# K sums of four heads in one piece with zero-padded remaining rows, the q phase by token tiles, and one weight block queued earlier

## The chip, the cores and the metric

The kernel runs on one core of one Trainium2 chip. The metric is the device time of one execution in microseconds (us); the time before is the median of three runs. TensorE is called PE, ScalarE ACT, VectorE DVE, GpSimd POOL, and SyncE SP (here only a DMA queue).

## The reference

Three stages in float32 follow each other (factors on the inputs left out):

```python
def phi(x):                                   # x: 4 batches, 8 heads, 576 tokens, 64
    h = x @ omega.T - sum(x * x) / 2          # 128 features
    return exp(h - max(h)) / sqrt(128)
q_p, k_p = phi(q * s), phi(k * s)
kv  = einsum('bhsm,bhsd->bhmd', k_p, v)       # the K sums; z = k_p summed over tokens
x   = (q_p @ kv) / (q_p @ z + 1e-06)          # 2304 tokens x 512 after joining the heads
g   = softplus(x @ w_in)                      # 512 -> 2048
y   = g @ w_out                               # 2048 -> 512
out = ((y @ w1) * (y @ w2)) @ w3 @ w_out2     # 512 -> 1024 -> 1024 -> 512
```

The kernel multiplies `w3 @ w_out2` first and applies the product to the tokens.

## The kernel before

All matrices are split into a high and a low part (`hi`, `lo`, type fp32r), and a product is three matmuls (`mm3`, L88 on). The attention's own sums are plain float32 matmuls, of which each shows as two instructions in the trace.

**K phase** (the loop over `i` in `range(2 * B)`, eight blocks of one batch and four heads). For each of four token tiles `t` of 128 tokens, `k_feat` projects four heads (six matmuls of 256 columns with `omh`, `oml`, named for the parts of omega), DVE takes the maxima (`nmax`, L312) and ACT the exponentials into `kp` (L317). The 576 tokens of a batch leave 64 rows over; those of two batches lie together in one tile `kpr` of 128 rows, even batches in rows 0 to 63 and odd ones in rows 64 to 127. `kv_sum(i, h)` sums one head of block `i`: four token tiles, in column halves of 64 (`matmul_half`), so eight float32 matmuls `ps<-vt,kp` of 128 rows x 64 columns, and then two matmuls `ps<-vrest,kpr` of 64 rows x 64 columns. Two heads of block `i - 1` are summed after `t = 2` and two after `t = 3`. The sums of four heads share a bank of PSUM and are copied to `kv` by ACT (L353).

**q phase** (the loop over `u`, a unit of one token tile and four heads; 36 units, 18 tiles). A unit takes: `q_feat` (the projection, `ps<-omh,qt`; exponentials one unit later), `q_turn` of the unit three before (four transposes `ps<-ident,qp`, copied to `qpt` by ACT, L373), `q_num` of the unit four before (eight float32 matmuls `ps<-kv,qpt` of 128 x 64, then `den`, its reciprocal and `xt` on DVE, L388 to L392), and in every second unit `x_turn` of an earlier tile (four transposes `ps<-ident,xt`, copied to `xs` by ACT and stored to `xd`). Between them `step` takes work from one queue, `queue`: the splitting of the next stage's weights, and of its tokens once they are stored (`operands`: casts such as `xs2h` on ACT, L433, sums and low parts on DVE).

**After it** come the up product (`widen` with `Up1`), the down product (`down`), the second up product (`Up2`), the weight product (`fold`, whose eight folds of 24 matmuls of 512 columns each need one block of w3, `made["w3", j]`, and all eight blocks of wo) and the last product (`narrow`).

The order on each engine is not that of the code: a scheduler places instructions by priority and by its own estimate of when operands are there. Every engine then works in that order. POOL makes the low parts of K and q (`split`, L266).

Of the kernel before, what the change touches and what calls it, by code (L numbers as in the profile page):

```python
# [19 lines left out]
F32 = mybir.dt.float32  # L20
# [7 lines left out]
B, H, S, D = 4, 8, 576, 64  # L28
M = 128
NT = B * S  # L30
DM, FF1, FF2 = 512, 2048, 1024
KD, NF, NJ = DM // 128, FF1 // 128, FF2 // 128
KT = 4
# [1 line left out]
BIAS = 896 * 16 * TOP  # L35
PSUM = bass.MemoryType.PSUM
DRAM = bass.MemoryType.DRAM
LQ = 3
LN = 1
XSLACK = 2  # L40
HALF = 64
PRE = 1
QBUF = 3
# [1 line left out]
QLAG = 1  # L45
N = 384
# [4 lines left out]
NG = NJ // 4  # L51
WSLOTS = 18
AHEAD = 4
JOB_Q = 0.9
# [10 lines left out]
def body(ctx: ExitStack, tc: tile.TileContext, q, k, k_rest, v, v_rest, om_t, w_in, w_out, w12, w3, wo, out):  # L65
# [10 lines left out]
    def ps():  # L76
        return ps_.tile([128, 512], F32, tag="ps", name="ps")
# [10 lines left out]
    def matmul(o, a, b, start, stop, **kw):  # L88
        nc.tensor.matmul(out=o, lhsT=a, rhs=b, start=start, stop=stop, **kw)  # L89
# [144 lines left out]
    def step(rate):  # L234
        due[0] += rate
        while due[0] > 0:
            if not pump_one():
                due[0] = min(due[0], 2.0)
                break
            due[0] -= 1  # L240
# [43 lines left out]
    def load_v(i):  # L284
        if i < 2 * B:
            vt[i] = K_.tile([128, KT, 4, D + 1], F32, tag="vt", bufs=3, name="vt")
            nc.sync.dma_start(out=vt[i], in_=v[i])

    def load_q(t):
        if t < NT // 128:  # L290
            raw[t] = Q_.tile([128, 512], F32, tag="rawq", bufs=4, name="rawq")
            nc.sync.dma_start(out=raw[t], in_=q[t])

    def split_q(t):
        if t < NT // 128:
            if len(qbuf) < QBUF:
                qbuf.append(Q_.tile([128, 2, 512], FR, name=f"qt{len(qbuf)}"))
            qt = qbuf[t % QBUF]
            split(qt[:, 0, :], qt[:, 1, :], raw[t])
            qts[t] = qt.rearrange("p x (c t) -> p x c t", c=4)  # L300
# [20 lines left out]
    def flush(n):  # L321
        while len(waiting) > n:
            waiting.pop(0)()
# [13 lines left out]

    def matmul_half(o, a, b, start, stop):
        for c in range(0, a.shape[-1], HALF):
            matmul(o[c:c + HALF], a[:, c:c + HALF], b, start, stop)  # L340

    def kv_sum(i, h):
        b, g = divmod(i, 2)
        if h == 0:
            if g == 0:
                kvs[b] = Q_.tile([128, H, D + 1], F32, name=f"kv{b}")
            kacc[i] = ps()[:, 0:4 * (D + 1)].rearrange("p (h d) -> p h d", h=4)
        for t in range(KT):
            matmul_half(kacc[i][:, h, :], kps[i][:, t, h, :], vt[i][:, t, h, :], t == 0, False)
        r, o = 2 * (b // 2) + g, 64 * (b % 2)  # L350
        matmul_half(kacc[i][:, h, :], kpr[r][o:o + 64, h, :], vrest[o:o + 64, r, h, :], False, True)
        if h == 3:
            nc.scalar.copy(out=kvs[b][:, 4 * g:4 * g + 4, :], in_=kacc.pop(i))  # L353

    qp, qpt, xt = {}, {}, {}

    def q_feat(u):
        t, g = divmod(u, 2)
        p = project(lambda p: [qts[t][:, x, 2 * g + p, :] for x in range(2)])

        def exps():
            qp[u] = M_.tile([128, 4, M], F32, tag="m", name="qp")
            features(*p, qp[u])

        waiting.append(exps)
        flush(QLAG)

    def q_turn(u):
        tp = ps()
        for h in range(4):  # L370
            nc.tensor.transpose(tp[:, 128 * h:128 * h + 128], qp[u][:, h, :], ident)  # L371
        qpt[u] = M_.tile([128, 4, 128], F32, tag="m", name="qpt")
        nc.scalar.copy(out=qpt[u], in_=tp.rearrange("p (h t) -> p h t", h=4))  # L373

    def q_num(u):
        t, g = divmod(u, 2)
        nm = ps()
        nm = nm[:, 0:4 * (D + 1)].rearrange("p (h d) -> p h d", h=4)
        lo, hi = 128 * t, 128 * t + 128
        for h in range(4):  # L380
            a = lo
            while a < hi:
                b = a // S
                e = min(hi, (b + 1) * S)
                matmul_half(nm[a - lo:e - lo, h, :], qpt[u][:, h, a - lo:e - lo], kvs[b][:, 4 * g + h, :], True, True)
                a = e
        den = sm.tile([128, 4, 1], F32, tag="den", name="den")
        nc.vector.tensor_scalar(out=den, in0=nm[:, :, D:D + 1], scalar1=1e-6 * M, scalar2=None, op0=ALU.add)  # L388
        nc.vector.reciprocal(out=den, in_=den)
        if g == 0:  # L390
            xt[t] = M_.tile([128, H, D], F32, tag="m", name="xt")
        nc.vector.tensor_tensor(  # L392
            out=xt[t][:, 4 * g:4 * g + 4, :], in0=nm[:, :, 0:D],
            in1=den.to_broadcast([128, 4, D]), op=ALU.mult,
        )

    def x_turn(t):
        tp = ps()
        x = xt[t].rearrange("p h d -> p (h d)")
        for c in range(KD):  # L400
            nc.tensor.transpose(tp[:, 128 * c:128 * c + 128], x[:, 128 * c:128 * c + 128], ident)  # L401
        xs = M_.tile([128, KD, 128], F32, tag="m", name="xs")
        nc.scalar.copy(out=xs, in_=tp.rearrange("p (c t) -> p c t", c=KD))
        nc.sync.dma_start(out=xd[:, :, 128 * t:128 * t + 128], in_=xs)
# [234 lines left out]
    split(*om_s, om)  # L639
    split_k(1)  # L640
    load_v(0)
    vrest = K_.tile([128, B, 4, D + 1], F32, name="vrest")
    nc.sync.dma_start(out=vrest, in_=v_rest)
    load_k(2)
    split_k(2)
    load_v(1)
# [2 lines left out]
    for i in range(2 * B):  # L649
        for t in range(KT):  # L650
            k_feat(i, t)
            if t == 0:
                load_k(i + 4)
            if t == 0 and i > PRE:
                split_k(i + 1)
            if t >= 2 and i:
                kv_sum(i - 1, 2 * t - 4)
                kv_sum(i - 1, 2 * t - 3)
            if t == KT - 1 and i:
                load_v(i + 2)  # L660
            if i == 2 * B - 1 and t < 2:
                split_q(t)
        if i % 4 == 0:
            for g in range(2):
                k_feat_rest(i // 2 + g)
        if i >= 2 * B - 3:
            load_q(i - (2 * B - 3))
    load_q(3)
    nq = 2 * NT // 128
    ln = LQ + LN  # L670
    lx = ln + XSLACK
    xo = {}
    for x in win[:2]:
        x.queue = nc.sync
    queue += job_ops(win[:2])
    for u in range(nq + lx + 2):
        if u >= LQ and u - LQ < nq:
            q_turn(u - LQ)
        if u >= nq:
            flush(max(0, QLAG - 1 - u + nq))  # L680
        if u == LQ:
            for h in range(4):
                kv_sum(2 * B - 1, h)
            kstack.close()
            pools["X0"] = ctx.enter_context(tc.tile_pool(name="X0", bufs=28, side="right", reuse_waits="tile"))
        if u >= ln and u - ln < nq:
            q_num(u - ln)
        if u >= lx and (u - lx) % 2 == 0:
            if (u - lx) // 2 < NT // 128:
                x_turn((u - lx) // 2)  # L690
                for c in range(2):
                    if (u - lx) // 2 == 2 * N // 128 * (c + 1) + 1:
                        xo[c], ops = operands(c, xd, "X0")
                        queue += ops
        if u < nq:
            q_feat(u)
            if u % 2:
                split_q(u // 2 + 2)
                load_q(u // 2 + 4)
        step(JOB_Q)  # L700
    until(lambda: 0 in ready)
    qstack.close()

# [106 lines left out]
    def wo_ops():  # L810
        ops = []
        for i in range(NJ):
            if i < NJ - 1:
                ops += halves(wof[i], 1, 2, "X1", lambda name: xslot("X1", 512, FR, name), ("wo", i))
            else:
                ops += halves(wof[i], 1, 0, None, lambda name: spare[name == "lo"], ("wo", i))
        return ops

    def w3_ops(j):
        return halves(w3f[j], 2, 2, "J", jt, ("w3", j))  # L820
# [206 lines left out]
    def after_2(c):  # L1027
        if c == 0:
            until(lambda: not queue)
            xn[0], ops = last_operands(0)  # L1030
            a, b = wo_ops(), w3_ops(0)
            queue.extend(b[:2] + a[:15] + b[2:] + a[15:] + ops)
        elif c == 1:
            free["X0"] -= 4
            free["W"] += 4
        else:
            free["X0"] -= 14
            free["W"] += 14

    widen(Up2, w12_j, ("X1", "X0", "X0"), after_2, lambda: None)  # L1040
    rows = {}
    order = [4 * g + 2 * h + e for g in range(NG) for e in range(2) for h in range(2)]
    for n, j in enumerate(order):
        if n + 1 < NJ:
            queue[:0] = w3_ops(order[n + 1])
        rows[j] = fold(j)
        if n % 2:
            queue[:0] = w34_ops(n // 2, rows[order[n - 1]], rows[j])
# [72 lines left out]
```

## Time and profile before

| | |
|---|---|
| median of 3 runs | 839.15 us (838.91 to 839.45) |
| the profiled execution | 840.52 us, of which its span is 838.7 us |
| PE busy | 823.8 us, 98% of the span |
| DVE, ACT, POOL busy | 593.5, 443.8 and 43.1 us |
| granted PE clock | full speed in every slice |
| K phase, q phase | about 4 to 61 us and 61 to 148 us of the span |

Busy time counts a matmul from its start to a modelled end, so neighbouring matmuls overlap. What one costs in a stream is the distance between two starts; this is how durations on PE are read below. A bracket such as [0.56 <-ACT xs1h L433] gives the idle time of the engine before the row and what ended it.

### The profile page before, as it was taken

The page shows a single profiled execution, that of the slowest core. Times are in us where ns is not written, and L with a number is a line of the kernel's source. Part 1 is how long each engine was busy: PE and PEld are TensorE (multiplying, and loading weights), DVE is VectorE, ACT ScalarE, POOL GpSimd, SP SyncE. Part 2 cuts the span into 40 slices and gives each one's busy share as a digit, 9 for nine tenths or more (in the row PEclk, how much of TensorE's full clock was granted, in tenths as well). Part 3 has the DMA queues.
Part 4 walks back from the last instruction along what each step waited for, and adds up shares of the span by engine and source line. Part 5 has one row for each costly group of instructions (what it writes and reads, how often), then busy time and mean ns, then how long its engine had stood idle before and what let it go on. Part 6 is the DMA issues. An engine that isn't in the chain of part 4 may idle for free.

```text
span 838.7 us, 14602 instructions
## 1 busy us (share of the span) xinstructions
PE 823.8 (98%) x5520; PEld 761.9 (91%) x5520; DVE 593.5 (71%) x1005; ACT 443.8 (53%) x863; POOL 43.1 (5%) x35
## 2 busy tenths in 40 slices
PE   8999999999999999999999999999999999999998
PEld 6888888989999999888888889999999997789998
DVE  4667888978676576765648834798887876978772
ACT  5688989566555566755645523332333223663440
POOL 3522331000000000000000000000000000000000
PEclk9999999999999999999999999999999999999999
DMA  8632354466534566778996623446455547153312
GB/s 298 225 130 76 105 176 139 148 214 211 205 129 147 188 222 223 249 249 266 308 314 228 216 67 96 176 146 208 181 216 214 185 144 259 68 172 111 103 67 75
DMA packets 75702, 150.05 MB, mean 179 GB/s; under 512 B 7152, under 2 KB 44656, under 8 KB 75632
## 3 DMA queue, kind: packets, MB, share of 16 engines
q1 hardware_dynamic: 64544, 101.94, 36.1%
q10 hardware_dynamic: 11088, 47.18, 16.5%
q8 instruction: 43, 0.70, 0.4%
q14 instruction: 27, 0.22, 0.1%
HBM read 98.24 MB, written 50.86 MB: 178 GB/s over the span
## 4 chain that ended last, share of the span: by engine, by line
PE 83%; DVE 7%; DMA 5%; ACT 2%; issue 1%; SPq 0%; ACTq 0%; DVEq 0%
PE ps L89 81%; DMA xq<-xd 1%; DVE s L925 1%; PE ps L371 1%; DMA xq<-pd 1%; DMA w3f<-f 1%; PE ps L401 1%; DMA raw<-in_w_in 1%; DVE s L426 1%; DVE f L141 1%; DMA wh<-wof 1%; DMA gd<-c 0%; DVE c L478 0%; DVE u L478 0%; DVE nmax L312 0%
## 5 line engine op out<-in xcount | busy, mean ns | idle before, releaser
L89 PE MATMUL ps<-dlo,hi 128*128 128x512 f32 (+1 forms) x320 | 117.7, 368 | 0.0
L89 PE MATMUL ps<-dhi,lo 128*128 128x512 f32 (+1 forms) x320 | 117.7, 368 | 0.0
L89 PE MATMUL ps<-dhi,hi 128*128 128x512 f32 (+1 forms) x320 | 117.5, 368 | 0.0
L586 DVE TENSOR_TENSOR dlo<-dn,dhi 128x512 fp32r<-128x512 f32 (+1 forms) x80 | 50.3, 634 | 48.3 <-ACT dhi L585 30.3
L585 ACT CAST dhi<-dn 128x512 fp32r<-128x512 f32 (+1 forms) x80 | 45.5, 575 | 54.8 <-DVE dlo L586 29.8
L478 DVE TENSOR_TENSOR c<-ps,u 128x384 f32<-128x384 f32 x144 | 71.5, 549 | 0.8
L478 DVE TENSOR_TENSOR u<-ps,p 128x384 f32<-128x384 f32 x48 | 26.6, 555 | 61.7 <-PE ps L89 57.4
L89 PEld LDWEIGHTS ps<-dhi,hi 128*128 128x128 f32 x320 | 60.3, 189 | 10.1
L89 PEld LDWEIGHTS ps<-dlo,hi 128*128 128x128 f32 x320 | 60.3, 189 | 10.0
L89 PEld LDWEIGHTS ps<-dhi,lo 128*128 128x128 f32 x320 | 60.3, 189 | 9.9
L131 ACT ACTIVATE f<-raw,bias 128x1024 f32<-128x1024 int16 (+2 forms) x43 | 46.3, 1083 | 37.6 <-DMA w3f<-f 9.4
L312 DVE TENSOR_REDUCE nmax<-ps 128x4 f32<-128x512 f32 x72 | 48.4, 683 | 21.0 <-PE ps L89 10.5
L511 ACT ACTIVATE c<-c 128x384 f32<-128x384 f32 x72 | 35.2, 525 | 49.8 <-DVE c L478 49.8
L135 DVE SCALAR_TENSOR_TENSOR f<-raw,f 128x1024 int32<-128x1024 f32 (+2 forms) x43 | 45.0, 1048 | 20.5 <-ACT raw L132 20.4
L485 ACT COPY p<-ps 128x384 f32<-128x384 f32 x48 | 22.8, 475 | 60.9 <-PE ps L89 45.4
L132 ACT ACTIVATE raw<-raw,bias 128x1024 f32<-128x1024 int16 (+2 forms) x43 | 46.3, 1084 | 0.5
L141 DVE SCALAR_TENSOR_TENSOR f<-raw,f 128x1024 int32<-128x1024 int32 (+2 forms) x43 | 46.0, 1069 | 0.5
L317 ACT ACTIVATE qp<-ps,nmax 128x128 f32<-128x128 f32 x144 | 41.8, 396 | 3.3 <-DVE nmax L312 3.1
L317 ACT ACTIVATE kp<-ps,nmax 128x128 f32<-128x128 f32 x128 | 35.4, 419 | 13.0 <-DVE nmax L312 12.9
L89 PE MATMUL ps<-omh,qt 128*128 128x256 f32 x144 | 34.7, 305 | 0.0
L89 PE MATMUL ps<-xs1h,thi 128*128 128x384 f32 x96 | 32.3, 336 | 1.2 <-DVE c L478 0.6
L89 PE MATMUL ps<-xs2l,thi 128*128 128x384 f32 x96 | 32.2, 335 | 0.6 <-DVE xs2l L436 0.6
(227 smaller groups left out, 2282.5 us busy)
## 6 DMA issues: line engine op xcount, KB each, us to landing
dn<-gd SPq DMA_DIRECT2D x64, 256.0 KB, 4.0
raw<-in_w ACTq DMA_DIRECT2D x16, 1023.8 KB, 6.3
gd<-c SPq DMA_DIRECT2D x80, 192.0 KB, 2.8
pd<-c SPq DMA_DIRECT2D x48, 192.0 KB, 2.5
raw<-in_w_out ACTq DMA_DIRECT2D x10, 767.8 KB, 4.3
raw<-in_w_in ACTq DMA_DIRECT2D x6, 1023.8 KB, 5.2
rawq<-in_q SPq DMA_DIRECT2D x18, 256.0 KB, 3.3
xd<-xs SPq DMA_DIRECT2D x18, 256.0 KB, 3.0
```

Of the source, the lines that this page charges most:

```text
L89: nc.tensor.matmul(out=o, lhsT=a, rhs=b, start=start, stop=stop, **kw)
L131: nc.scalar.activation(out=self.f, in_=top, func=AF.Relu, scale=TOP, bias=bias[:, 0:1])
L132: nc.scalar.activation(out=self.words(1, F32, 2), in_=top, func=AF.Identity, scale=TOP, bias=bias[:, 1:2])
L135: nc.vector.scalar_tensor_tensor(out=self.f.bitcast(I32), in0=self.words(1, F32, 2), scalar=-2.0 ** 31, in1=self.f, op0=ALU.max, op1=ALU.min)
L141: nc.vector.scalar_tensor_tensor(out=fi, in0=self.words(0, I32, 2), scalar=13, in1=fi, op0=ALU.logical_shift_right, op1=ALU.bitwise_or,)
L312: nc.vector.tensor_reduce(out=nmax, in_=pj, axis=AX.X, op=ALU.max, negate=True)
L317: nc.scalar.activation(out=dst[:, h, :], in_=pj[:, h, :], func=AF.Exp, bias=nmax[:, h:h + 1])
L478: nc.vector.tensor_tensor(out=z, in0=bank, in1=y, op=ALU.add)
L485: nc.scalar.copy(out=p6, in_=b1)
L511: nc.scalar.activation(out=dst, in_=src, func=AF.Softplus)
L585: nc.scalar.copy(out=hi, in_=got[m])
L586: nc.vector.tensor_tensor(out=lo, in0=got.pop(m), in1=hi.bitcast(F32), op=ALU.subtract)
```

## The change

It has three parts. (1) `kv_sum(i)` sums all four heads of a block at once, after `t = 3`, as one accumulation group of the bank. `vrest` gets a copy for each parity of the batch in which the other parity's 64 rows are zero (two POOL memsets and two DMAs of 64 rows in place of one of 128), and the remaining rows are then multiplied with all 128 rows. (2) The q phase goes by whole token tiles: turns of the tile two before between the two projections, then both `q_num` of that tile, then `x_turn` of the tile three before. (3) The second w3 block of the weight product is queued with the first, behind all of wo; the loop no longer puts it at the queue's head.

```diff
-LQ = 3
-LN = 1
-XSLACK = 2
+TLAG = 2
+XLAG = 3
...
-            matmul(o[c:c + HALF], a[:, c:c + HALF], b, start, stop)
-
-    def kv_sum(i, h):
+            matmul(o[c:c + HALF], a[:, c:c + HALF], b, start, stop, skip_group_check=True)
+
+    def kv_sum(i):
         b, g = divmod(i, 2)
...
+        acc = ps()[:, 0:4 * (D + 1)].rearrange("p (h d) -> p h d", h=4)
+        for h in range(4):
+            for t in range(KT):
+                matmul_half(acc[:, h, :], kps[i][:, t, h, :], vt[i][:, t, h, :], h == 0 and t == 0, False)
+            r = 2 * (b // 2) + g
+            matmul_half(acc[:, h, :], kpr[r][:, h, :], vrest[:, b % 2, r, h, :], False, h == 3)
+        nc.scalar.copy(out=kvs[b][:, 4 * g:4 * g + 4, :], in_=acc)
...
-    vrest = K_.tile([128, B, 4, D + 1], F32, name="vrest")
-    nc.sync.dma_start(out=vrest, in_=v_rest)
+    vrest = K_.tile([128, 2, B, 4, D + 1], F32, name="vrest")
+    for x in range(2):
+        nc.gpsimd.memset(vrest[64 * (1 - x):64 * (2 - x), x], 0.0)
+        nc.sync.dma_start(out=vrest[64 * x:64 * x + 64, x], in_=v_rest[64 * x:64 * x + 64])
...
-            if t >= 2 and i:
-                kv_sum(i - 1, 2 * t - 4)
-                kv_sum(i - 1, 2 * t - 3)
             if t == KT - 1 and i:
+                kv_sum(i - 1)
                 load_v(i + 2)
...
-    for u in range(nq + lx + 2):
-        if u >= LQ and u - LQ < nq:
-            q_turn(u - LQ)
...
+    for t in range(nt + XLAG):
+        for g in range(2):
+            if 0 <= t - TLAG < nt:
+                q_turn(2 * (t - TLAG) + g)
+            if t < nt:
+                q_feat(2 * t + g)
+            else:
+                flush(0)
+            step(JOB_Q)
+        if t < nt:
+            split_q(t + 2)
+            load_q(t + 4)
+        if t == 1:
+            kv_sum(2 * B - 1)
...
+        if 0 <= t - TLAG < nt:
+            for g in range(2):
+                q_num(2 * (t - TLAG) + g)
+        if t >= XLAG:
+            x_turn(t - XLAG)
...
-            a, b = wo_ops(), w3_ops(0)
-            queue.extend(b[:2] + a[:15] + b[2:] + a[15:] + ops)
+            a, b = wo_ops(), w3_ops(order[0])
+            queue.extend(b[:2] + a[:15] + b[2:] + a[15:] + w3_ops(order[1]) + ops)
...
-        if n + 1 < NJ:
+        if 0 < n < NJ - 1:
             queue[:0] = w3_ops(order[n + 1])
```

How the instructions move on PE in the K phase: first the end of a block before (`omh,kt2h` and the like are the projection, `vt,kp` and `vrest,kpr` the sums of two heads; each row counts matmuls).

```order
L89 MATMUL ps<-omh,kt2l 128x256
L89 MATMUL ps<-vt,kp 64x65 x8
L89 MATMUL ps<-vrest,kpr 64x65 x2
L89 MATMUL ps<-vt,kp 64x65 x8
L89 MATMUL ps<-vrest,kpr 64x65 x2
L89 MATMUL ps<-omh,kt2h 128x256
```

Now the sums of four heads stand together behind the fourth projection of a block. In the block with `kt2`, though, the scheduler put one `vt,kp` by itself among the projections, and moved the matmuls with the low part `kt2l` behind those with `kt2h`:

```order
L88 MATMUL ps<-omh,kt2h 128x256
L88 MATMUL ps<-oml,kt2h 128x256
L88 MATMUL ps<-vt,kp 64x65
L88 MATMUL ps<-omh,kt2l 128x256
L88 MATMUL ps<-omh,kt2h 128x256
L88 MATMUL ps<-oml,kt2h 128x256
L88 MATMUL ps<-omh,kt2l 128x256 x2
```

So PE turns from projections to sums once in a block instead of twice, and once more in that block for the single matmul.

On PE in the q phase, one tile before (`ident,qp` and `ident,xt` are the transposes, `kv_282,qpt` the sums of `q_num`):

```order
L371 MATMUL ps<-ident,qp 128x128 x4
L89 MATMUL ps<-kv_282,qpt 64x65 x8
L89 MATMUL ps<-omh,qt_994 128x256
L89 MATMUL ps<-oml,qt_994 128x256
L89 MATMUL ps<-omh,qt_994 128x256 x2
L89 MATMUL ps<-oml,qt_994 128x256
L89 MATMUL ps<-omh,qt_994 128x256
L371 MATMUL ps<-ident,qp 128x128 x4
L89 MATMUL ps<-kv_282,qpt 64x65 x8
L401 MATMUL ps<-ident,xt 128x128 x4
```

and with the change:

```order
L88 MATMUL ps<-omh,qt_880 128x256
L88 MATMUL ps<-oml,qt_880 128x256
L88 MATMUL ps<-omh,qt_880 128x256 x2
L88 MATMUL ps<-oml,qt_880 128x256
L88 MATMUL ps<-omh,qt_880 128x256
L88 MATMUL ps<-kv_298,qpt 64x65 x16
L399 MATMUL ps<-ident,xt 128x128 x4
L369 MATMUL ps<-ident,qp 128x128 x4
```

The 16 sums of a tile now follow its second projection in one piece, and the second turn of the same tile stands only one projection ahead of them.

On ACT behind the q phase, where the operands of the third group of 768 tokens are cast (`xs3h`, `xs1h`) and the next weights are unpacked (`f<-raw`, whose `raw` a DMA brings), before:

```order
L485 COPY p_2800<-ps 128x384
L433 CAST xs3h<-s_2739 128x768
L131 ACTIVATE f<-raw,bias 128x1024
L433 CAST xs1h<-s_2717 128x768
L132 ACTIVATE raw<-raw,bias 128x1024
```

and with the change:

```order
L509 ACTIVATE c_2790<-ps 128x384
L483 COPY p_2803<-ps 128x384
L431 CAST xs1h<-s_2720 128x768
L130 ACTIVATE f<-raw,bias 128x1024
L431 CAST xa12h<-xq 128x768
```

The cast `xs1h` no longer stands behind the unpacking that waits for a DMA.

## Rows read from the trace of the kernel before

**Rows 1.** Windows: length, busy us of PE, PEld, DVE, ACT, POOL; clock, DMA share, GB/s.
```profile
18.98:61.34 42.36, 42.36 (x637) 37.21 (x633) 26.37 (x38) 33.60 (x118) 16.11 (x9) 1.00 0.54 183
76.28:86.71 10.43, 9.22 (x114) 7.72 (x113) 10.36 (x27) 7.40 (x24) 1.80 (x2) 1.00 0.36 102
86.71:108.27 21.56, 21.56 (x281) 19.20 (x280) 17.55 (x49) 19.08 (x56) 7.20 (x6) 1.00 0.50 149
108.27:118.37 10.10, 9.54 (x114) 7.83 (x113) 8.48 (x22) 9.58 (x27) 2.39 (x2) 1.00 0.63 208
118.37:139.97 21.60, 21.60 (x282) 19.17 (x281) 19.23 (x50) 20.79 (x60) 5.36 (x4) 1.00 0.34 100
```

**Rows 2.** The chain that ended last, from its one long piece on PE.
```profile
174.55 451.47 PE ps L89 x2424
```

**Rows 3.** Timeline of PE, K phase: start us, us, engine, line, operation, instructions.
```profile
21.23 0.28 PE L89 MATMUL ps<-omh,kt2l 128*128 128x256 f32 x1
21.44 0.69 PE L89 MATMUL ps<-vt,kp 128*64 128x65 f32 x16
22.06 0.33 PE L89 MATMUL ps<-vrest,kpr 64*64 64x65 f32 x4
22.32 0.69 PE L89 MATMUL ps<-vt,kp 128*64 128x65 f32 x16
...
23.20 0.39 PE L89 MATMUL ps<-omh,kt2h 128*128 128x256 f32 x1
23.42 0.28 PE L89 MATMUL ps<-oml,kt2h 128*128 128x256 f32 x1
23.54 0.28 PE L89 MATMUL ps<-omh,kt2l 128*128 128x256 f32 x1
```

**Rows 4.** Timeline of POOL: its one 128x128 memset, and the second K split.
```profile
0.73 0.20 POOL masks.py:197 MEMSET ident<- 128x128 f32 x1 [0.29 <-POOLq L1109]
...
16.92 2.36 POOL L266 TENSOR_TENSOR kt2l<-rawk,kt2h 128x1024 fp32r<-128x1024 f32 x1 [2.38 <-DVE kt2h L265]
```

**Rows 5.** Timeline of PE: the first turn among the last K sums, first and last.
```profile
63.56 0.33 PE L371 MATMUL ps<-ident,qp 128*128 128x128 f32 x1
...
66.03 0.69 PE L89 MATMUL ps<-vt,kp 128*64 128x65 f32 x16
```

**Rows 6.** Timeline of PE, q phase: a return to the projection, and the last tiles.
```profile
131.95 0.39 PE L89 MATMUL ps<-omh,qt 128*128 128x256 f32 x1
132.17 0.28 PE L89 MATMUL ps<-oml,qt 128*128 128x256 f32 x1
...
142.55 0.66 PE L401 MATMUL ps<-ident,xt 128*128 128x128 f32 x4
143.04 0.60 PE L371 MATMUL ps<-ident,qp 128*128 128x128 f32 x4
...
145.39 0.66 PE L401 MATMUL ps<-ident,xt 128*128 128x128 f32 x4
145.98 0.69 PE L89 MATMUL ps<-kv,qpt 128*64 128x65 f32 x16
148.23 0.44 PE L401 MATMUL ps<-ident,xt 128*128 128x128 f32 x2 [1.56 <-DVE xt L392]
```

**Rows 7.** Timeline of ACT: one tile of the q phase with a cast.
```profile
138.20 0.96 ACT L433 CAST xa22h<-xq 128x768 fp32r<-128x768 f32 x1
...
142.52 1.23 ACT L317 ACTIVATE qp<-ps,nmax 128x128 f32<-128x128 f32 x4
```

**Rows 8.** Timeline of PE: the last wait ahead of the long piece.
```profile
174.55 0.45 PE L89 MATMUL ps<-xs1h,thi 128*128 128x384 f32 x1 [0.56 <-ACT xs1h L433]
```

**Rows 9.** Timeline of SP's queue and of ACT: second w3 block, last wo block.
```profile
699.78 0.93 SPq L785 DMA_DIRECT2D wh<-w3f  x2
700.75 0.43 SPq L785 DMA_DIRECT2D wh<-wof  x1
...
705.20 0.62 ACT L794 CAST spare<-wh 128x512 fp32r<-128x512 f32 x1 [0.87 <-DMA wh<-wof]
```

More of the change, by code (lines that the diff above doesn't have):

```diff
@@ L339, in matmul_half @@
         for c in range(0, a.shape[-1], HALF):
-            matmul(o[c:c + HALF], a[:, c:c + HALF], b, start, stop)
-    def kv_sum(i, h):
+            matmul(o[c:c + HALF], a[:, c:c + HALF], b, start, stop, skip_group_check=True)
+    def kv_sum(i):
         b, g = divmod(i, 2)
[L344 to L353, printed above, removed]
+        if g == 0:
+            kvs[b] = Q_.tile([128, H, D + 1], F32, name=f"kv{b}")
+        acc = ps()[:, 0:4 * (D + 1)].rearrange("p (h d) -> p h d", h=4)
[5 more added lines that the diff above has]
+        nc.scalar.copy(out=kvs[b][:, 4 * g:4 * g + 4, :], in_=acc)
     qp, qpt, xt = {}, {}, {}
@@ L668, in body @@
     load_q(3)
-    nq = 2 * NT // 128
-    ln = LQ + LN
-    lx = ln + XSLACK
     xo = {}
@@ L675, in body @@
     queue += job_ops(win[:2])
-    for u in range(nq + lx + 2):
-        if u >= LQ and u - LQ < nq:
-            q_turn(u - LQ)
[L679 to L683, printed above, removed]
+    nt = NT // 128
+    for t in range(nt + XLAG):
[12 more added lines that the diff above has]
+            kv_sum(2 * B - 1)
             kstack.close()
             pools["X0"] = ctx.enter_context(tc.tile_pool(name="X0", bufs=28, side="right", reuse_waits="tile"))
[L686 to L700, printed above, removed]
+        if 0 <= t - TLAG < nt:
[3 more added lines that the diff above has]
+            x_turn(t - XLAG)
+            for c in range(2):
+                if t - XLAG == 2 * N // 128 * (c + 1) + 1:
+                    xo[c], ops = operands(c, xd, "X0")
+                    queue += ops
     until(lambda: 0 in ready)
@@ L1038, in after_2 @@
             free["W"] += 14
+    order = [4 * g + 2 * h + e for g in range(NG) for e in range(2) for h in range(2)]
     widen(Up2, w12_j, ("X1", "X0", "X0"), after_2, lambda: None)
     rows = {}
-    order = [4 * g + 2 * h + e for g in range(NG) for e in range(2) for h in range(2)]
     for n, j in enumerate(order):
-        if n + 1 < NJ:
+        if 0 < n < NJ - 1:
             queue[:0] = w3_ops(order[n + 1])
```

## The prediction

> **What bounds the kernel now.** I read the page first (98% of the span is PE), then the chain of waits. From 174.55 us on the chain is one piece of matmuls, 451 us long [rows 2]: what PE saves ahead of that point arrives whole at its end, and the diff touches nothing between there and the weight product. So the question is how fast PE gets through the K and q phases. The windows [rows 1] part them. In the K phase PE is busy all of the 42.36 us, ACT for 33.6 and DVE for 26.4: PE alone sets the pace. In the q phase, windows are cut where the sums of a tile's second unit start. Five tiles take 21.56 us (86.71 to 108.27) and five 21.60 (118.37 to 139.97), 4.32 a tile, with PE never idle; but ACT is busy for 19.08 and then 20.79 of it. Two windows of two tiles take 10.43 and 10.10 in place of 8.64: 1.79 and 1.46 lost, the first with DVE busy for 10.36.
>
> Within a phase I read starts on PE's timeline. In [rows 3] two projections start 0.12 apart (23.42 to 23.54); sixteen `vt,kp` instructions take 0.62, 0.039 each; four `vrest,kpr` take 0.26 where four of the others would take 0.155. Going from projections to sums costs 0.21 - 0.12 = 0.09 (21.23 to 21.44), going back 0.22 - 0.12 = 0.10 (23.20 to 23.42). The kernel pays for changes of shape, and the change makes fewer of them.
>
> **Part by part.** The sum is made against the profiled execution, 840.52 us; the median is 839.15, so 1.37 is taken off at the end.
>
> *Remaining rows with 128 rows.* Same instructions, same columns, but now of the shape of their neighbours. 32 heads x (0.26 - 0.155) = -3.4 [rows 3]. Ends: 0 if the 0.26 is not due to the 64 rows, -3.4.
>
> *Four heads in one piece.* Seven blocks (those summed inside the loop) lose one way out and back, 0.19: -1.3 [rows 3]. Ends -1.0 to -1.5, by the reading error of a start.
>
> *Memsets, the DMA and the single matmul.* No row has a memset of 64x1040. The bounds are the one of 128x128, 0.20, and the 128x1024 subtraction, 2.36 [rows 4]; I take 1, below the middle, since the first is the same kind of instruction. POOL has 2.38 idle ahead of the `kt2l` split, so either end is hidden there. The second DMA only takes a place in SP's queue some 11 us before what follows is used. But DVE now casts `kt2h` one maximum (0.61) later, so `kt2l` is ready at 16.92 + 0.6 + 2.36 = 19.9. PE begins this block at 18.98 (where the first window of [rows 1] is cut), 0.61 earlier by the two terms above, has eight projections and the single matmul to do and gets to `kt2l` about 19.5: a wait of 0.4. With the single `vt,kp` (a way out and back, 0.2): +0.6. Ends +0.2 and +1.2.
>
> *The first turn out of the last K sums.* From 63.56 to 66.03 [rows 5], 2.47, lie four transposes (at most 0.49, [rows 6], 142.55 to 143.04), 16 `vt,kp` (0.62) and 4 `vrest,kpr` (0.26): 1.10 went on crossings between them. One way out and back stays: -0.9. Ends -0.6 to -1.1.
>
> *q phase by tiles.* Before, a tile goes twice from transposes to sums (0.59 - 0.49 = 0.10, [rows 6]), once from sums to projections (131.95 to 132.17, 0.10) and once from sums to transposes; with the change once from projections to sums (0.09) and once to transposes. Per tile 0.30 - 0.09 = 0.21. Only where PE sets the pace does this come out. A tile with a cast takes 4.32 on ACT, one instruction behind the other (138.20 to 142.52, [rows 7]), which is what it takes on PE; ACT's new order has a cast in each of the four tiles near the end of the phase, so these gain nothing. Of the four disturbed tiles the first two are DVE's (10.36 of 10.43): nothing. In the other two DVE is not full (8.48 of 10.10), and `x_turn` now comes two units behind its `xt` instead of one, so I let half of the 1.46 go: -0.7. Ten tiles x 0.21 = -2.1. Together -2.8; ends 0 (ACT everywhere) and -3.8 - 3.25 = -7.0 (PE everywhere, disturbances gone).
>
> *End of the phase.* The last two tiles have no projections left to cover the copies of their turns; the row at 148.23 shows 1.56 idle there already, for `xt` [rows 6]. I put these equal. Behind it, `xs1h` no longer waits behind the unpacking of weights on ACT: the 0.56 of [rows 8] goes, -0.5. Ends -0.9 and +1.2 (one transpose-and-copy more for each of two tiles, 0.6 each).
>
> *Weight product.* The three transfers are issued at the same three places of the queue; the last wo block moves up by 0.97 and the w3 pair back by about 0.45 [rows 9]. The first fold, which needed the wo block (cast at 705.20), ends earlier, the second starts later. Taken as 0; ends -1.0 and +0.5.
>
> Sum: -3.4 - 1.3 + 0.6 - 0.9 - 2.8 - 0.5 + 0 = -8.3. Profiled: 832.2; median: 839.15 - 8.3 = **830.9**.
>
> **Rivals.** *Disturbances absorbed* (chance 0.18). Turns run three units behind their exponentials instead of two, `x_turn` two behind `xt`: enough for DVE's bursts. For it: in 86.71 to 108.27 DVE is at 81% without PE ever waiting. Against: DVE's 10.36 of 10.43. All 18 tiles gain (-3.8) and most of the 3.25 goes (-2.6): -11.9, 827.2.
>
> *ACT sets the pace of the q phase* (0.20). Its 20.79 of 21.60 us [rows 1] speaks for it, 19.08 of 21.56 against. The phase gains nothing: -5.5, 833.6.
>
> *The remaining rows are not cheaper* (0.08). Then the 0.26 comes from the change of operands and not from the 64 rows; PE's 0.10 for other changes of shape speaks against: -4.9, 834.2. The Trainium skill ("TensorE: Matmul & The Clock Gate", Part 3) goes further: products on different row or column groups run at the same time, so the two halves of a small product would overlap and padding would throw this away. By that rule four instructions take two steps, an estimate of 0.078, padding costs 32 x 0.077 = 2.5, and the time is 836.7. The trace disagrees: 0.26 is more than four steps, not fewer.
>
> *Slower* (0.04): the sums of a tile now need the copy of a turn that stands one projection ahead of them, where they had a whole unit before. If ACT reaches that copy late in each tile, because exponentials in front of it wait for DVE's maxima, each tile loses what a disturbed one loses now, (1.79 + 1.46) / 4 = 0.8. The q term is then 18 x 0.8 - 3.25 = +11.2 in place of -2.8, the sum +5.7 and the time 844.9. It decides from 5.5 / 18 = 0.3 us a tile. Against it: ACT is idle for 2.5 of 21.56 us in the first quiet window, so it is seldom that late.
>
> **How the numbers follow.** The forecast's case has 0.50. A measurement of this kernel can tell 0.2%, 1.7 us. All cases but the last lie over 1.7 below 839.15: 0.94 faster; 0.02 same, for a forecast or rival whose bounds all fall high; 0.04 slower. The range reaches from the absorbed case with a little of its lower bound (826.0) to the unchanged q phase with `kt2l` and the tail at their dear ends (836.0).
>
> **What would show it.** In the profile after: four `vrest,kpr` in 0.155 us (the first term); blocks of the K phase 0.6 shorter; the end of the K phase some 4 us earlier; quiet tiles of 4.1 in the q phase and 4.3 where ACT has a cast; the long piece on PE starting near 166. It is wrong if tiles stay at 4.3 throughout with ACT full, if four `vrest,kpr` still take 0.26, or if PE waits for `qpt` ahead of the sums in most tiles.

## The result, and the profile after

The changed kernel takes 832.1 us (median of 4 runs, 831.43 to 832.73), beside 839.03 us of the kernel before in the same session: the ratio is 0.9919 (95% interval 0.9902 to 0.9937), so 6.8 us less. The profiled execution took 832.73 us with a span of 830.9 us, 7.8 less than the 838.7 before. The forecast for the median was 830.9, 8.3 less. The total is nearly right, but the two profiles show that its parts are not.

The first view is that of the windows, cut where the same matmuls start in both kernels: the K phase from the first projection with `kt1h` to the first q projection, and the q phase to the first matmul of the up product (the columns are those of [rows 1]). With the change:

```profile
10.82:53.12 42.30, 41.38 (x738) 39.22 (x736) 29.33 (x43) 35.26 (x128) 21.77 (x14) 1.00 0.74 263
53.12:140.03 86.91, 77.28 (x1091) 71.11 (x1087) 76.53 (x190) 80.76 (x226) 21.59 (x15) 1.00 0.40 120
```

And the same two in the kernel before:

```profile
12.00:61.34 49.34, 49.34 (x739) 43.32 (x737) 31.90 (x47) 39.22 (x140) 20.72 (x13) 1.00 0.60 213
61.34:148.42 87.08, 83.75 (x1090) 72.51 (x1087) 71.79 (x184) 77.40 (x215) 20.59 (x15) 1.00 0.40 121
```

This K phase takes 42.30 instead of 49.34 us, 7.0 less, where the forecast had about 3.6 by that point (28 of the 32 heads at 0.105, 1.3 for the crossings, 0.6 back at `kt2l`). The first q projection starts 8.2 earlier (53.12 instead of 61.34), but 1.2 of that lay already at the first projection with `kt1h`, ahead of every sum. In the ten profiles with this K part that projection starts anywhere from 10.39 to 11.92, while the way from it to the first q projection takes 42.3 to 42.6 in all of them: the 7.0 belong to the kernel, the 1.2 can belong to the execution. The q phase, from which the forecast took another 4 or so, takes 86.91 instead of 87.08. In it PE works 6.5 us less (83.75 to 77.28), and 6.3 of that are idle time now.

Why K gained so much stands on PE's timeline of the changed kernel, at the last four heads:

```profile
56.17 0.69 PE L88 MATMUL ps<-vt,kp 128*64 128x65 f32 x16
56.68 0.29 PE L88 MATMUL ps<-vrest,kpr 128*64 128x65 f32 x4
56.80 0.64 PE L88 MATMUL ps<-vt,kp 128*64 128x65 f32 x16
57.27 0.29 PE L88 MATMUL ps<-vrest,kpr 128*64 128x65 f32 x4
57.38 0.64 PE L88 MATMUL ps<-vt,kp 128*64 128x65 f32 x16
```

Four `vrest,kpr` take 0.12 now (56.68 to 56.80), as forecast or a little less. But the sixteen `vt,kp`, whose instructions did not change at all, take 0.51 and then 0.47, where they took 0.62 [rows 3]. Four heads go from twice 1.76 us (21.44 to 23.20 in [rows 3]) to 2.48 (56.17 to 58.65, where the next transpose starts). A block is 1.2 shorter (29.31 to 34.85, 5.54; before 32.60 to 39.36, 6.76), except two: that with `kt2`, where PE waits 0.74 for `kt2l` and goes out and back once more, gains 0.1 (16.57 to 23.35; before 18.98 to 25.86), and the next one, where it waits 0.19 for `kt1l`, gains 0.8 (to 29.31; before to 32.60).

The waits show what the q phase does with what it won. PE's waits after (what it waited for, us in total, times, longest):

```profile
PE ps L88 <- ACT qpt L371: 7.6, 12, 1.7
PE ps L88 <- DMA rawk<-in_k: 4.0, 1, 4.0
PE ps L399 <- DVE den L387: 1.8, 1, 1.8
PE ps L88 <- DVE c L476: 1.8, 2, 1.5
PE ps L88 <- ACT hi L790: 1.2, 1, 1.2
PE ps L88 <- POOL kt2l L265: 0.7, 1, 0.7
```

The first row is new: the sums wait for the copy of their own tile's turn, 12 times. On PE's timeline these waits lie in three places, at the entry (62.88, 64.40), in the middle where operands are loaded (103.69 among others), and in the last tiles:

```profile
62.88 0.69 PE L88 MATMUL ps<-kv,qpt 128*64 128x65 f32 x16 [1.70 <-ACT qpt L371]
64.40 0.69 PE L88 MATMUL ps<-kv,qpt 128*64 128x65 f32 x16 [0.83 <-ACT qpt L371]
...
103.69 0.69 PE L88 MATMUL ps<-kv,qpt 128*64 128x65 f32 x16 [0.83 <-ACT qpt L371]
...
133.84 0.69 PE L88 MATMUL ps<-kv,qpt 128*64 128x65 f32 x16 [0.84 <-ACT qpt L371]
136.28 1.17 PE L88 MATMUL ps<-kv,qpt 128*64 128x65 f32 x32 [0.29 <-ACT qpt L371]
139.86 0.41 PE L399 MATMUL ps<-ident,xt 128*128 128x128 f32 x2 [1.82 <-DVE den L387]
```

ACT's timeline says why at the first two places. The transposes of the first turn run from 58.65 to 59.31, but their copy runs at 62.24, behind twelve exponentials, a weight cast and a copy of `kv` in ACT's order; and in the middle ACT stands for a DMA, with the copies of two finished transposes behind it:

```profile
57.61 3.29 ACT L316 ACTIVATE qp<-ps,nmax 128x128 f32<-128x128 f32 x12
61.02 1.04 ACT L179 CAST thi<-t 128x1024 fp32r<-128x1024 f32 x1
61.97 0.37 ACT L351 COPY kv<-ps 128x260 f32<-128x260 f32 x1
62.24 0.59 ACT L371 COPY qpt<-ps 128x512 f32<-128x512 f32 x1
...
100.31 0.83 ACT L431 CAST xa11h<-xq 128x768 fp32r<-128x768 f32 x1 [0.90 <-DMA xq<-xd]
101.05 0.58 ACT L401 COPY xs<-ps 128x512 f32<-128x512 f32 x1
101.53 0.59 ACT L371 COPY qpt<-ps 128x512 f32<-128x512 f32 x1
```

Last, the granted clock. It fell to 0.50 (1.2 GHz) behind the last of these waits: in the windows of the changed kernel PE idles for 1.82 of 137.40 to 140.00, and from about 140.6 on it runs three us at half speed.

```profile
137.40:140.00 2.60, 0.78 (x8) 0.58 (x7) 2.60 (x8) 1.17 (x2) 0.00 (x0) 1.00 0.23 65
141.00:144.00 3.00, 3.00 (x12) 2.90 (x11) 2.58 (x3) 1.99 (x4) 0.00 (x0) 0.50 0.00 0
```

Matmuls of the up product stand 0.32 apart there (140.63, 140.95, 141.27) instead of 0.17, and the lead over the kernel before falls from 8.4 us at 140.03 to 6.9 at 143.94. It comes back to 9.0 by 175 us, because PE no longer waits for `xs2l` (0.60 idle before, the lead grows by 0.9 there) and `xs1h` (0.56, [rows 8], by 1.0 there); 1.4 are lost again by 638.78 at two waits for `c` in the down product.

### The profile page after: what moved, and what is told of

It reads as the page before. It is cut to its first block, busy times and chain, and to the rows that moved or that the text cites. A ratio compares the mean times of both kernels' runs of the same rounds, so it can differ in the third digit from the quotient of the medians.

```text
span 830.9 us, 14593 instructions
## 1 busy us (share of the span) xinstructions
PE 808.8 (97%) x5520; PEld 757.2 (91%) x5520; DVE 595.9 (72%) x1005; ACT 443.7 (53%) x863; POOL 46.1 (6%) x37
## 5 line engine op out<-in xcount | busy, mean ns | idle before, releaser
L316 ACT ACTIVATE qp<-ps,nmax 128x128 f32<-128x128 f32 x144 | 43.9, 462 | 1.2 <-DVE nmax L311 1.2
L88 PE MATMUL ps<-xs3l,thi 128*128 128x384 f32 x96 | 32.6, 339 | 0.0
```

Source lines behind the costliest of these rows:

```text
L316: nc.scalar.activation(out=dst[:, h, :], in_=pj[:, h, :], func=AF.Exp, bias=nmax[:, h:h + 1])
```

## The experiments

Each kernel was timed against the kernel before on the same chip. The experiments ask three things: what made the K sums cheap, what holds the q phase, and what the low clock and the third part are worth.

**Padding alone.** The kernel before, still two heads at a time:

```diff
-        r, o = 2 * (b // 2) + g, 64 * (b % 2)
-        matmul_half(kacc[i][:, h, :], kpr[r][o:o + 64, h, :], vrest[o:o + 64, r, h, :], False, True)
+        r = 2 * (b // 2) + g
+        matmul_half(kacc[i][:, h, :], kpr[r][:, h, :], vrest[:, b % 2, r, h, :], False, True)
```

> The kernel before with the zero-padded remaining rows alone; still two heads at a time, the q phase and the weight product as before. Theory 1, a change of shape is paid on both sides: the 64-row instructions make the vt,kp next to them dear too, so with padding sixteen vt,kp fall from 0.62 to about 0.47 us and four vrest,kpr from 0.26 to 0.12; a head costs 0.59 instead of 0.88, 32 heads give 9.3 and the time is about 830. Theory 2, the prediction's: only the four remaining instructions were dear and the sixteen stay at 0.62 here; 32 x 0.105 = 3.4 and about 835.7.

Measured: 839.15 us, ratio 0.9996 (0.9986 to 1.0006). The mechanism is theory 1's: sixteen `vt,kp` take 0.47 and four `vrest,kpr` 0.12, without any other change of the code. But no time came out of it. In pieces of two heads, each with its own way out and back, a piece takes 1.31 us instead of 1.76 (24.04 to 25.35; before 24.10 to 25.86), so the 14 pieces of the K phase bring 6.3, less than theory 1 counted. From the first projection with `kt1h` the phase is 3.3 shorter (11.44 to 57.45). In the block with `kt2` 1.8 are lost (waits of 0.21 for `kt2h` and 1.15 for `kt2l`, and the way back to the projection), and 1.1 where ACT's exponentials, no longer covered, are waited for in front of the sums (0.3 for `kp`, 0.3 for `kpr`). The rest goes in the q phase, 89.77 us long here. Its first turn waits 1.6 for exponentials, and behind that the clock falls:

```profile
57.45:147.22 89.77, 84.54 (x1090) 73.47 (x1087) 73.80 (x187) 80.44 (x223) 20.57 (x15) 0.98 0.39 117
62.00:68.00 6.00, 6.00 (x90) 5.42 (x89) 0.07 (x1) 4.57 (x13) 0.27 (x1) 0.72 0.15 46
```

**Four heads in one piece alone**, with 64-row products:

```diff
-            if t >= 2 and i:
-                kv_sum(i - 1, 2 * t - 4)
-                kv_sum(i - 1, 2 * t - 3)
             if t == KT - 1 and i:
+                for h in range(4):
+                    kv_sum(i - 1, h)
```

> The kernel before with the sums of four heads in one piece behind the fourth projection, the remaining rows still multiplied with 64 rows. Theory 1: sixteen vt,kp stay at 0.62 us, only seven ways out and back of 0.19 go: -1.3, about 837.8. Theory 2, one long piece makes the vt,kp cheap: sixteen take about 0.47, 32 x 0.15 = 4.8 and with the 1.3 together -6.1, about 833.

Measured: 838.99 us, ratio 0.9995 (0.9985 to 1.0005). On PE's timeline the instructions cost what they did before, so theory 2 is out:

```profile
22.74 0.69 PE L89 MATMUL ps<-vt,kp 128*64 128x65 f32 x16
23.36 0.33 PE L89 MATMUL ps<-vrest,kpr 64*64 64x65 f32 x4
23.62 0.69 PE L89 MATMUL ps<-vt,kp 128*64 128x65 f32 x16
```

A block is shorter by the 0.19 that was forecast (from the end of the sums of one block at 32.57 to that of the next at 39.14 it takes 6.57 us; before, between the same places of two blocks, 29.68 to 36.44, 6.76). The time shows even less, since PE waits 0.6 for `kt2l` here too: from the first projection with `kt1h` the K phase is 0.5 shorter.

So the two shapes of the rows are what counts: the tile printed behind the names changes from 128*64 to 64*64 and back with each head. The starts of single instructions show where the price lies. They come in pairs, and inside a row the next pair follows 0.058 later. Around the four `vrest,kpr` of the kernel before they start so (each row is one pair):

```profile
21.90 0.23 PE L89 MATMUL ps<-vt,kp 128*64 128x65 f32 x2
22.06 0.27 PE L89 MATMUL ps<-vrest,kpr 64*64 64x65 f32 x2
22.17 0.23 PE L89 MATMUL ps<-vrest,kpr 64*64 64x65 f32 x2
22.32 0.28 PE L89 MATMUL ps<-vt,kp 128*64 128x65 f32 x2
```

Each change comes 0.10 late, and the second pair behind it 0.05 late (0.11 instead of 0.058): about 0.15 a change, on either side. The 0.62 of sixteen `vt,kp` held one of them, and the instructions of 64 rows are not dear in themselves. The Trainium skill states the mechanism ("TensorEngine Tiling (Array Packing)", Tiling Modes, Key Properties): changing the tiling mode drains TensorE. The trace agrees, with these 0.15.

**The whole K part alone**, q phase by units:

> The kernel before with the whole K part (padding and four heads at once), the q phase by units and the weight product as before. If the K part alone brought the gain of the change, the first projection after the K phase comes 8 us earlier (53.3 instead of 61.34), the long piece on PE starts near 166.5, and the time is 831 to 832, that of the change. If the prediction's split is right (4.1 from K sums, the rest from the q phase) it is about 835.

Measured: 836.13 us, ratio 0.9964 (0.9952 to 0.9977), so -3.0: near the second case by its time, but not by its mechanism. The first q projection is as early as the first case has it, 52.80, and from the first projection with `kt1h` the K phase takes 42.4. The q phase takes 4.3 back, as the windows show:

```profile
52.80:144.14 91.34, 85.75 (x1091) 74.30 (x1087) 75.32 (x189) 81.24 (x226) 20.60 (x15) 0.96 0.38 115
58.00:64.00 6.00, 6.00 (x80) 4.96 (x81) 0.91 (x2) 4.07 (x12) 0.21 (x1) 0.50 0.12 46
```

At the first turn PE waits 2.6 for exponentials, and then the last K sums run at 1.2 GHz. What PE saves ahead of the q phase does not all arrive behind it: the first projection is 8.5 earlier than before, but ACT starts the exponentials of the first unit only 5.9 earlier (57.25 instead of 63.14), and PE waits for the difference.

**The q phase by tiles alone**, K sums as before:

> The kernel before with the q phase by tiles alone. If the waits for qpt and the low clock at its end gave back what the fewer changes of shape bring, the time is 838 to 840 and PE waits for qpt some ten times, 5 to 8 us in all. By the prediction (-0.9, -2.8 and -0.5) it is about 835.

Measured: 836.0 us, ratio 0.9961 (0.9947 to 0.9975), -3.3. The waits for `qpt` are there as expected (10 of them, 5.4 us), and in the phase itself little is won:

```profile
60.90:147.04 86.14, 78.39 (x1090) 71.62 (x1087) 74.09 (x186) 76.94 (x215) 19.89 (x15) 1.00 0.41 122
```

86.14 instead of 87.08. What I had not expected is the rest: behind the phase the lead grows from 1.4 us at the first up matmul to 4.5 in the first folds, since the casts of the third token group come earlier and PE no longer waits for `xs2l`, `xs1h` and `c`. So each part alone brings about 3, and both together about 7 to 9. Whether the two are worth more than their sum of 6.3 these runs leave open. The waits at the entry are as long in the changed kernel (1.70 and 0.83) as with the K part alone (2.56), but there the last K sums run ahead of the first turn, and its profile has no low clock behind these waits.

**PE kept at work in the last wait**: the changed kernel with sums that nobody reads behind the last `num`.

```diff
                 q_num(2 * (t - TLAG) + g)
+            if t - TLAG == nt - 1:
+                fl = ps()[:, 0:4 * (D + 1)].rearrange("p (h d) -> p h d", h=4)
+                for _ in range(4):
+                    for h in range(4):
+                        matmul_half(fl[:, h, :], qpt[2 * nt - 1][:, h, :], kvs[B - 1][:, 4 + h, :], True, True)
```

> The changed kernel with 32 more sums of 64 columns behind the last num (the last unit's product repeated into a bank that nobody reads), so that PE works instead of idling ahead of the last x_turn (1.82 us idle in the changed kernel, granted clock 0.50 right behind it). If that idling is what brings the low clock, the granted clock stays at 1.00 from 138 to 146, the first matmuls of the up product stand 0.17 apart instead of 0.32, and the time falls by about 1.5, to 830.6. If the low clock comes from the waits before it or from the start of the 384-column matmuls themselves, it stays, and the time is 832 to 833.

Measured: 831.92 us, ratio 0.9911 (0.9896 to 0.9925): the time did not fall by 1.5. The clock stayed full where the idling was filled, but fell behind the two waits at the entry, where the changed kernel's profile had it full:

```profile
64.00:70.00 6.00, 5.86 (x69) 5.59 (x70) 4.66 (x14) 5.59 (x17) 1.27 (x1) 0.72 0.15 44
138.00:146.00 8.00, 7.20 (x101) 6.60 (x97) 7.57 (x14) 5.28 (x9) 0.00 (x0) 1.00 0.32 89
```

So one profile does not tell where the low clock will be in the next execution. The changed kernel run again (below) had none at either place. That filling the gap is what kept the clock up is therefore not shown.

**Two other orders of the q phase.** In the first both turns stand ahead of both projections, in the second the sums come a tile later:

```diff
             if 0 <= t - TLAG < nt:
                 q_turn(2 * (t - TLAG) + g)
+        for g in range(2):
             if t < nt:
```

> The changed kernel with both turns of a tile ahead of its two projections, so that the second turn stands two projections ahead of the sums instead of one; nothing else moves. Theory, the short distance makes the new waits: the 7.6 us of waits for qpt fall to under 2, and one crossing a tile less: 4 to 7 us less, 825 to 828. Rival, ACT is the bound of the q phase (80.8 busy of 86.9 us): the waits only change their name (for qp at the turns), the phase stays 85 to 87 us, 831 to 832.5.

```diff
-        if 0 <= t - TLAG < nt:
+        if 0 <= t - NLAG < nt:
             for g in range(2):
-                q_num(2 * (t - TLAG) + g)
+                q_num(2 * (t - NLAG) + g)
```

(with `NLAG = 3` and `XLAG = 4`)

> The changed kernel with the sums of a tile one tile later (and x_turn one later still), so that a copy of a turn has a whole tile of about 4 us before it is read. Theory of the short distance: no waits for qpt in the middle of the phase, quiet tiles 4.0, the end one tile's latency longer (about +1 us): 826 to 829. Rival, ACT is the bound: tiles stay at 4.7 on average, 832 to 834.

Turns first: 829.91 us, ratio 0.9886 (0.9873 to 0.9899). The waits for `qpt` fall only from 7.6 to 6.0 us (9 instead of 12), so the short distance was not their main cause; the phase takes 85.6. Sums late: 835.51 us, 0.9959 (0.9945 to 0.9973), slower than the changed kernel. There the waits for `qpt` are all but gone (0.6 in all) and the phase takes 83.55 us, the shortest of all, but other waits come, for `den` and `xt` in the phase and for casts and low parts behind it:

```profile
PE ps L89 <- DVE den L388: 2.1, 1, 2.1
PE ps L89 <- ACT xs2h L432: 1.8, 1, 1.8
PE ps L400 <- DVE xt L391: 1.5, 2, 1.3
PE ps L89 <- ACT xs3h L432: 1.3, 1, 1.3
PE ps L89 <- DVE xs2l L435: 1.3, 1, 1.3
```

PE comes to the products of the third token group before their casts `xs2h` and `xs3h`, and the clock is at 0.58 from 162 to 168 in that profile. `xs2h` is late because DVE's sum for it is: DVE starts these sums at 159.10, when their operands land, and the load is issued at 154.90, behind five stores `gd<-c` on SP's queue, where the changed kernel issues it at 147.75, ahead of those stores. `xs3h` then stands on ACT behind a copy that waits 3.8 for PE.

**The weight blocks as before**, alone and with the turns first, and the changed kernel again:

```diff
-            a, b = wo_ops(), w3_ops(order[0])
-            queue.extend(b[:2] + a[:15] + b[2:] + a[15:] + w3_ops(order[1]) + ops)
+            a, b = wo_ops(), w3_ops(0)
+            queue.extend(b[:2] + a[:15] + b[2:] + a[15:] + ops)
...
-        if 0 < n < NJ - 1:
+        if n + 1 < NJ:
```

> The changed kernel with the weight blocks queued as before. The prediction takes the third part of the change at nothing (-1.0 to +0.5): 831 to 833. If queueing the second w3 block earlier is worth something it is over 833, with a wait for lo or hi of the second fold that the changed kernel does not have.

> The changed kernel with both turns of a tile ahead of its two projections and the weight blocks queued as before. If the earlier second w3 block is what makes PE wait 1.8 us for c in the down product (it is not waited for in the run with the weight blocks as before), this takes about 1 off the run with the turns first alone: 828 to 829. If that wait only moves elsewhere, 829.5 to 830.5.

> The changed kernel again, on the chip of the two runs above, so that the part of the weight blocks and that of the turns can be read against it: 831.5 to 832.5. Its low clock stretch may lie elsewhere than in the profile shown, behind the first waits for qpt (about 64 to 69) or behind the last x_turn (140 to 144), or be missing.

| kernel | median us | ratio to before (95% interval) |
|---|---|---|
| changed, first session | 832.1 | 0.9919 (0.9902 to 0.9937) |
| changed, again | 830.46 | 0.9881 (0.9862 to 0.9899) |
| weight blocks as before | 831.45 | 0.9907 (0.9894 to 0.9920) |
| turns first | 829.91 | 0.9886 (0.9873 to 0.9899) |
| turns first, weight blocks as before | 830.3 | 0.9876 (0.9857 to 0.9896) |

The third part of the change is worth nothing that these runs can tell, and of the turns' order no more can be said. I had read the 1.8 us of waits for `c` as the price of the earlier block. That reading fell: the changed kernel's second profile has no such wait, and none of the low clock at the same place either; the same instructions run at full speed there.

```profile
53.44:140.31 86.87, 77.33 (x1091) 71.11 (x1087) 76.51 (x190) 80.47 (x226) 21.61 (x15) 1.00 0.41 120
141.00:144.00 3.00, 3.00 (x20) 2.97 (x19) 3.00 (x5) 2.81 (x5) 0.00 (x0) 1.00 0.15 39
```

Its span is 828.6 us against 830.9, with the same K and q phases (from the first projection with `kt1h` 42.31 and 42.30, the q phase 86.87 and 86.91). What the two profiles agree on belongs to the kernel; the 1.5 us of low clock and the waits for `c` belong to the execution. Why `c` came late in one and not in the other stays open.

**Casts on POOL**, with turns first and weight blocks as before:

```diff
-                nc.scalar.copy(out=o[name][0], in_=x())
+                (nc.gpsimd.tensor_copy if src is xd and c < 2 else nc.scalar.copy)(out=o[name][0], in_=x())
```

> As the run before it in this call, and the 14 casts of the first two operand groups (0.84 to 1.0 us each on ACT, some 12 in all) on POOL, which is idle for 65 of the 86 us of the q phase. If ACT's sum sets the length of the q phase, tiles with a cast fall from 4.26 to 4.0, the waits for qpt shrink to under 3 us and the phase is 3 to 6 us shorter: 823 to 827. If the waits come from the order on ACT and from DVE's maxima, the phase keeps its 85 us: 828 to 830. POOL and DVE may also disturb each other, which could make it slower.

Measured: 829.28 us, ratio 0.9869 (0.9845 to 0.9892), the lowest of all, but not told apart from the run without it (0.9876). ACT is relieved by 5.9 us (79.86 without it), and the q phase keeps its length (85.44 without it):

```profile
53.72:139.30 85.58, 76.18 (x1090) 70.31 (x1087) 78.39 (x193) 74.01 (x217) 31.05 (x27) 1.00 0.41 122
```

With ACT at 74.01 of 85.58 us, PE at 76.18 and DVE at 78.39, no engine's sum sets this phase. It is a chain across engines that each work in a fixed order, and time is lost where one of them stands for something that the others do not need. One such place is left on DVE here: it waits 0.58 for the operands' DMA between two `den`, and the tile takes 5.06 us from `x_turn` to `x_turn` (102.47 to 107.53). The relief had a price, though: DVE works 2.5 us more (75.87 without it). Its operations on two 128x768 operands take 0.93 to 0.96 where POOL is idle and up to 1.80 where POOL works (`xs3l` at 117.37). So this run does not show what less work on ACT alone would bring.

**The first operations behind that DMA on POOL too**:

```diff
-                nc.vector.tensor_tensor(out=s[name], in0=x(), in1=y(), op=op_)
+                (nc.gpsimd if src is xd and c == 0 and name in ("a11", "s1", "s2") else nc.vector).tensor_tensor(out=s[name], in0=x(), in1=y(), op=op_)
...
-                nc.vector.tensor_tensor(out=o[name][1], in0=x(), in1=o[name][0].bitcast(F32), op=ALU.subtract)
+                (nc.gpsimd if src is xd and c == 0 and name == "a11" else nc.vector).tensor_tensor(out=o[name][1], in0=x(), in1=o[name][0].bitcast(F32), op=ALU.subtract)
```

> As the run with the casts on POOL, and the three operations of the first operand group that stand first behind its DMA (the low part xa11l and the two sums s) moved from DVE to POOL, so that neither ACT nor DVE stands in front of that DMA. In the run with the casts on POOL the tile in which this happens takes 5.06 us between its x_turns, with DVE waiting 0.58 for the DMA between two den. If an engine that waits in its own order for a DMA is what holds PE there, that tile falls to 4.0 to 4.3 and the time by about 0.8, to 828.5. If the tile stays near 5, the wait comes from elsewhere, and the time is 829 to 830.

Measured: 835.5 us, ratio 0.9961 (0.9948 to 0.9973), 6 to 8 slower than the run it was made from. The tile in question did fall to 3.97, as the first theory has it (PE's transposes of `x_turn`):

```profile
98.31 0.66 PE L399 MATMUL ps<-ident,xt 128*128 128x128 f32 x4
102.28 0.66 PE L399 MATMUL ps<-ident,xt 128*128 128x128 f32 x4
106.25 0.66 PE L399 MATMUL ps<-ident,xt 128*128 128x128 f32 x4
116.81 1.12 PE L399 MATMUL ps<-ident,xt 128*128 128x128 f32 x4
```

And the next one took 10.56. On DVE's timeline, the low part `xs2l` stands ahead of the maxima and the cast of the next tile, and now waits for POOL, whose two sums take 2.42 and 1.82 where DVE takes about 0.95:

```profile
109.92 1.54 DVE L434 TENSOR_TENSOR xs2l<-s,xs2h 128x768 fp32r<-128x768 f32 x1 [4.50 <-POOL xs2h L431]
111.39 1.27 DVE L311 TENSOR_REDUCE nmax<-ps 128x4 f32<-128x512 f32 x2
```

PE then waits 4.8 for the next `qt`, and the clock is at 0.50 from 112 to 116. The mechanism is the one named, in both directions: whoever stands in an engine's order for a slow producer holds all that is behind it.

## Why the prediction was right, and where it was not

The total was right by luck: two errors of 3 to 4 us met, 7.0 instead of 3.6 gained in the K phase and 0.2 instead of 4.1 in the q phase. By its own steps:

- *Remaining rows with 128 rows, -3.4*: the mechanism was right, the size was not. The step that failed is "sixteen `vt,kp` instructions take 0.62, 0.039 each". The 0.62 held the change to the 64-row shape at its end; without it they take 0.47. A head saves 0.26 (3.52 - 2.48 over four heads), not 0.105, so the term is 32 x 0.26 = -8.3, of which 28 heads, -7.3, fall into the K phase. "The kernel pays for changes of shape" stood in the same paragraph, and I did not apply it to the row beside it.
- *Four heads in one piece, -1.3*: seven times 0.19, shown by the run with that edit alone (6.76 to 6.57 a block).
- *Memsets, `kt2l`, the single matmul, +0.6*: it was +1.6. The memset of 64x1040 took 0.96 us (I had taken 1), the wait for `kt2l` 0.74 (forecast 0.4); the block with `kt2` lost 1.1, and the next, with its wait for `kt1l` that the sum does not have, 0.5. With -7.3 and -1.3 that makes the 7.0 measured.
- *First turn out of the last K sums (-0.9) and q phase by tiles (-2.8)*: PE's own work did fall as forecast and more (quiet tiles 4.0, forecast 4.1; tiles with a cast 4.26, forecast 4.3). But the phase won 0.2, not 4. The step that failed is "only where PE sets the pace does this come out", applied tile by tile, with no term for the places where PE enters and leaves the phase. PE's idle time in it rose from 3.3 to 9.6 us (87.08 - 83.75 and 86.91 - 77.28): 2.5 at the entry, 3.5 in the last two tiles, 3.4 between. "I put these equal", of the last two tiles, was wrong by 2 (3.5 instead of the 1.56 at 148.23).
- *The rivals on this*: that ACT sets the pace had the result of the phase (no gain); the reason is not borne out, since 6 us less on ACT changed nothing, though DVE took 2.5 more in that run. The wait of the sums for a turn that stands too close, priced as the slower case, did come, 12 times in 9 of the 18 tiles and 7.6 us; it did not decide, since it took only what PE had saved. The text named "PE waits for `qpt` ahead of the sums in most tiles" as a sign of being wrong. For the q term it was one.
- *The remaining rows are not cheaper*: out. Four 64-row instructions took 0.26, four padded ones take 0.12, and their neighbours became cheaper too. By the Trainium skill ("TensorE: Matmul & The Clock Gate", Part 3) products on different row or column groups run at the same time. "The trace disagrees" was read from the 0.26, which the changes of shape made: in both shapes, before and after, the instructions start in pairs 0.007 apart, so padding took nothing away there. Which two products make a pair no row shows.
- *End of the phase, -0.5*: the wait for `xs1h` is gone, and so is that for `xs2l` (0.60), which I had not counted; the run with the tile order alone shows some 3 us gained behind the phase. In the profiled execution the low clock took 1.5 of it and the waits for `c` another 1.4; in the second profile they did not.
- *Weight product, 0*: nothing that the runs can tell.

## What to carry to other kernels

When a matmul's shape alternates, the price of the change lies partly in the rows of its neighbours: compare the same instruction in a stream without the change before dividing a row by its count. A phase in which PE is busy all the time is not yet bound by PE: before counting savings through it, look at the engine that is next in line at its entry and at its end, and at who stands in that engine's order ahead of what PE needs. And a difference below 2 us between two profiles of one execution each may be the execution's own: a second profile of the same kernel showed which, and a window cut at the same matmul in both keeps a late start out of the comparison.

## What was not expected of the hardware

- A pair of changes between 128*64 and 64*64 matmuls costs about 0.3 us, as much as ten of the small instructions at 0.029 each.
- The granted clock fell to 0.50 behind single waits of PE of 1.6 to 2.6 us, and stayed there for 3 us and more with PE busy throughout; behind similar waits in another execution of the same kernel it did not fall. Such a stretch cost about 1.5 us in the changed kernel, and the K part alone had one of over 6 us behind its first turn.
- POOL's subtractions and sums of 128x768 took 1.8 to 2.4 us where DVE, with POOL idle, takes about 0.95; a cast of that size took 0.82 on POOL at best, as on ACT, and up to 1.57. The two disturb each other: every such operation of DVE in the two runs with casts on POOL that took over 1.0 us ran beside work on POOL (up to 2.08), and every cast of POOL that took 1.5 or more ran beside one of DVE's.
